# Turning three small vectors into rows with the matrix engine before they are written to DRAM

## The chip, the cores and the metric

The kernel runs on 1 core of one Trainium2 chip. The metric is the device time of one execution in microseconds (us); lower is better. The kernel was tuned already.

## The reference, cut to what matters

The program is a transformer block whose normalisations and residual additions are scaled and shifted by a condition vector `c`: linear attention, then a gated feed-forward net (S = 2048 tokens, D = 1024, F = 3584).

```python
mod = (silu(c) @ w_mod).reshape(1, 6, 1, D)
sa, ca, ga, sb, cb, gb = (mod[:, i] for i in range(6))
h = layernorm(x) * (1 + ca) + sa
x = x + ga * A(h, wqkv, wo)          # A: linear attention; it uses z = sum over the tokens of phi(k)
h = layernorm(x) * (1 + cb) + sb
x = x + gb * B(h, w_gate, w_up, w_down)   # B: silu(h @ w_gate) * (h @ w_up) @ w_down
```

Three vectors of 1024 numbers matter here: `ga`, `gb` and `z`. Each is computed as columns (element 128 m + p on partition p, column m), but is needed as one row that is repeated on all 128 partitions.

## The kernel before

A vector goes from columns to a repeated row by way of DRAM: write the 128x8 columns, wait until they have landed, read the row back with a broadcast. All DMAs are issued by one queue, that of the sync engine (SP), in program order; `wait_for("sp", ...)` makes that queue stand.

```python
def mod_cols(c0, first=None):                 # column sums: 16 matmuls of one column, into bank 6
    for m in range(NDT):
        for i in range(2):
            P.pe("matmul", out=PS[:, 6, c0 + m:c0 + m + 1], lhsT=MHL[:, i, m * 128:(m + 1) * 128],
                 rhs=ONES[:, 0:1], start=mcol_first[0], stop=(i == 1), skip_group_check=True)
            mcol_first[0] = False

def z_mm(st):                                 # z is summed in bank 6 too
    for hg in range(NHG):
        P.pe("matmul", out=PS[:, 6, 32 + hg:33 + hg], ...)   # arguments cut

def mod_fin_row(c0, i, dst):
    P.dve("tensor_copy", out=MROW[:, i, :], in_=PS[:, 6, c0:c0 + 8])
    wr = P.dma("mdw%d" % i, MDR[i].rearrange("(m p) -> p m", p=128), MROW[:, i, :], allow_slow_non_contiguous=True)
    P.wait_for("sp", [wr])
    P.dma("mdr%d" % i, dst[:], MDR[i].unsqueeze(0).to_broadcast([128, D]))
# ... cut: phases that project q and k. ga is made in the last of their four chunks:
add(s3, 2, lambda: mod_cols(0))
add(s3, 5, lambda: mod_fin_row(0, 0, GA_B))
# ... then z
P.dve("tensor_copy", out=ZCOL[:], in_=PS[:, 6, 32:40])
zw = P.dma("zw", ZDR[0].rearrange("(g p) -> p g", p=128), ZCOL[:], allow_slow_non_contiguous=True)
P.wait_for("sp", [zw])
P.dma("zr", ZB[:], ZDR[0:1, :].to_broadcast([128, D]))
P.dma("wo", WO[:], wov)
# ... cut. The first chunk (of four) of the feed-forward net:
for ft in range(NFT):                         # 28 steps of 16 matmuls, 3.45 us each
    q = 14 * ch + ft // 2
    # 8 matmuls with GUG[q % 4], 8 with GUU[q % 4], then the activation and the product (cut)
    if ft % 2 == 1 and q + 4 < 14 * NCH:
        gu_load(q + 4)                        # 1 MB of gate/up weights into the buffer just freed
    if ch == 0 and ft % 2 == 0 and ft < 14:
        P.dma("wd%d" % (ft // 2), ...)        # 1 MB of down weights (arguments cut)
    if ch == 0 and ft == 3:
        mod_cols(8)
        mod_fin_row(8, 1, GB_B)               # gb; first used after ft 27
```

Four gate/up buffers turn over: the load issued after step ft (odd) is used first in step ft + 7, some 20 us later. A helper makes an engine that touches a PSUM bank wait for the last use of that bank by every other engine.

## Time and profile before

| | before |
|---|---|
| time, median of the first 3 runs | 847.46 us (847.26 to 847.69) |
| the execution that the profile shows | 850.55 us, span 848.2 us |
| TensorE (PE) busy | 98% of the span |
| write of gb, issue to landing | 18.0 us for 2 KB |
| write of ga, issue to the next issue | 13.8 us for 2 KB |
| write of z, issue to landing | 10.4 us for 4 KB |

The second row of the table deserves a look: the execution in the profile took 3 us longer than the timed runs. I shall come back to it.

From the page of before: its span, the busy time, share and count of instructions of each engine, and the shares of the engines in the chain of work that ended last.

```profile
span 848.2 us, 10377 instructions
...
PE 835.3 (98%) x4287; PEld 385.3 (45%) x4287; DVE 296.1 (35%) x624; ACT 211.7 (25%) x363; POOL 39.7 (5%) x51
...
PE 93%; DMA 4%; DVE 2%; SPq 0%; issue 0%; POOL 0%; ACT 0%; DVEq 0%; ACTq 0%
...
```

PE is the limit nearly everywhere, so what counts is where PE stands. The waits of PE in before give the waiting engine, whom it waited for, the total, the number of waits and the longest.

```profile
...
PE ps L178 <- DMA guu_115<-in_B_w_up_dram: 5.4, 1, 5.4
...
PE ps L178 <- DVE mrow L178: 1.3, 1, 1.3
...
```

These are the only waits for the parts that the change touches. The first is for a gate/up load. Here is the sync queue of before in order of time (start, time to issue, what was issued):

```profile
...
273.20 0.86 SPq L178 DMA_DIRECT2D mod_row<-mrow  x1
291.20 0.34 SPq L178 DMA_DIRECT2D gb_b<-mod_row  x1
...
292.12 0.45 SPq L966 DMA_DIRECT2D gug_111<-in_B_w_gate_dram  x1
292.61 4.38 SPq L966 DMA_DIRECT2D guu_115<-in_B_w_up_dram  x1
...
```

The write of gb is issued at 273.20 us, just after the load of ft 3, and the queue issues nothing more until 291.20. The gate/up load after ft 5, which PE allowed near 278.6 us, when it was through with ft 5, is issued at 292.12. The timeline of PE shows what comes of it; in brackets is the idle time just before and its releaser:

```profile
...
297.56 1.89 PE L178 MATMUL ps<-h2t,guu_114 128*128 128x512 bf16 x8
304.82 3.59 PE L178 MATMUL ps<-h2t,gug_111 128*128 128x512 bf16 x8 [5.37 <-DMA guu_115<-in_B_w_up_dram]
308.21 2.19 PE L178 MATMUL ps<-h2t,guu_115 128*128 128x512 bf16 x8
310.24 1.89 PE L178 MATMUL ps<-h2t,gug_111 128*128 128x512 bf16 x8
...
```

PE idles 5.37 us. After that eight matmuls take 3.59 us, where eight take 1.89 us before and later. The stretch from 299 to 313 us of before, in the view by windows (length; busy time and instructions of PE, its weight loads, VectorE, ScalarE and GpSimd; granted clock; share of the DMA engines; GB/s):

```profile
...
299.00:313.00 14.00, 8.63 (x32) 3.35 (x30) 1.37 (x2) 1.19 (x2) 0.00 (x0) 0.76 1.12 333
...
```

The granted clock was 0.76. From the start of the group at 297.56 to the end of this disturbance the loss is 7.5 us: the ends of groups overlap with the next, and undisturbed a group of eight starts every 1.727 us, so these 32 matmuls should take 6.91 us from start to start and take 14.40 (297.56 to 311.96). The second wait, for the copy of ga out of bank 6, is 1.29 us long in PE's timeline of before:

```profile
...
115.31 3.61 PE L178 MATMUL ps<-wqk,ht 128*128 128x512 bf16 x16
120.21 0.25 PE L178 MATMUL ps<-ones,pk_87 128*128 128x1 bf16 x4 [1.29 <-DVE mrow L178]
...
```

The small matmuls at 120.21 us add to z in bank 6. They may not go on until VectorE has copied ga's columns out of the same bank, and VectorE has that copy behind other work.

### The profile page before, as it was taken

The page shows a single profiled execution, that of the slowest core. Times are in us where ns is not written, and L with a number is a line of the kernel's source. Part 1 is how long each engine was busy: PE and PEld are TensorE (multiplying, and loading weights), DVE is VectorE, ACT ScalarE, POOL GpSimd, SP SyncE. Part 2 cuts the span into 40 slices and gives each one's busy share as a digit, 9 for nine tenths or more (in the row PEclk, how much of TensorE's full clock was granted, in tenths as well). Part 3 has the DMA queues.
Part 4 walks back from the last instruction along what each step waited for, and adds up shares of the span by engine and source line. Part 5 has one row for each costly group of instructions (what it writes and reads, how often), then busy time and mean ns, then how long its engine had stood idle before and what let it go on. Part 6 is the DMA issues. An engine that isn't in the chain of part 4 may idle for free.

```text
span 848.2 us, 10377 instructions
## 1 busy us (share of the span) xinstructions
PE 835.3 (98%) x4287; PEld 385.3 (45%) x4287; DVE 296.1 (35%) x624; ACT 211.7 (25%) x363; POOL 39.7 (5%) x51
## 2 busy tenths in 40 slices
PE   8999999999999979999999999999999999999998
PEld 4544444444444434444444444444444444444444
DVE  4677966476984211111122111112211112122111
ACT  5677753223333111110111110111111101111101
POOL 1000000000050000020000002000000200000000
PEclk9899999999999989999999999999999999999999
DMA  9792321877195299540255554025555303553000
GB/s 311 221 315 50 67 80 14 222 205 260 39 249 183 36 338 293 155 112 26 63 149 149 149 152 115 19 85 158 156 156 154 67 26 106 149 148 100 1 25 25
DMA packets 176462, 113.00 MB, mean 133 GB/s; under 512 B 35616, under 2 KB 159648, under 8 KB 176416
## 3 DMA queue, kind: packets, MB, share of 16 engines
q1 hardware_dynamic: 176416, 112.35, 47.5%
q8 instruction: 33, 0.54, 0.3%
q14 instruction: 13, 0.11, 0.1%
HBM read 100.67 MB, written 4.33 MB: 124 GB/s over the span
## 4 chain that ended last, share of the span: by engine, by line
PE 93%; DMA 4%; DVE 2%; SPq 0%; issue 0%; POOL 0%; ACT 0%; DVEq 0%; ACTq 0%
PE ps L178 93%; DMA mod_row<-mrow 2%; DMA guu_115<-in_B_w_up_dram 1%; DMA xres<-in_A_x_dram 1%; DVE acc L178 0%; DVE xres L178 0%; SPq L966 0%; SPq L178 0%; DVE mhl L178 0%; POOL rstd L178 0%; DVE stats L178 0%; DVE mv L178 0%; ACT mw L178 0%; ACT e_92 L178 0%; DVE ve L178 0%
## 5 line engine op out<-in xcount | busy, mean ns | idle before, releaser
L178 DVE TENSOR_TENSOR at<-sg,ps 128x512 bf16<-128x512 bf16 x112 | 77.0, 688 | 305.3 <-PE ps L178 305.3
L178 ACT ACTIVATE sg<-ps 128x512 bf16<-128x512 f32 x112 | 66.9, 597 | 318.4 <-PE ps L178 318.4
L178 PE MATMUL ps<-wd_a,at 128*128 128x512 bf16 (+2 forms) x528 | 115.9, 373 | 0.0
L178 PE MATMUL ps<-wd_b,at 128*128 128x512 bf16 (+2 forms) x396 | 88.3, 373 | 0.0
L178 PEld LDWEIGHTS ps<-wd_a,at 128*128 128x128 bf16 x528 | 51.1, 98 | 59.8
L178 DVE TENSOR_TENSOR ut<-att,gb_b 128x512 bf16<-128x512 bf16 (+1 forms) x32 | 14.5, 454 | 164.8 <-ACT att L178 164.8
L178 ACT ACTIVATE att<-ps 128x512 bf16<-128x512 f32 (+1 forms) x32 | 19.0, 594 | 179.7 <-PE ps L178 179.7
L178 PE MATMUL ps<-h2t,gug_111 128*128 128x512 bf16 x224 | 54.6, 388 | 5.4 <-DMA guu_115<-in_B_w_up_dram 5.4
L178 PE MATMUL ps<-ht,wqk 128*128 128x512 bf16 x256 | 59.1, 387 | 0.0
L178 PEld LDWEIGHTS ps<-wd_b,at 128*128 128x128 bf16 x396 | 38.3, 98 | 44.7
L178 PE MATMUL ps<-wqk,ht 128*128 128x512 bf16 x256 | 58.5, 384 | 0.0
L178 PE MATMUL ps<-mw,pqt 128*128 128x512 bf16 x256 | 56.2, 379 | 0.1
L178 PE MATMUL ps<-h2t,guu_115 128*128 128x512 bf16 x224 | 53.2, 381 | 0.0
L178 PE MATMUL ps<-h2t,guu_113 128*128 128x512 bf16 x224 | 52.9, 379 | 0.0
L178 PE MATMUL ps<-h2t,gug_110 128*128 128x512 bf16 x224 | 52.9, 379 | 0.0
L178 PE MATMUL ps<-h2t,guu_114 128*128 128x512 bf16 x224 | 52.9, 379 | 0.0
L178 PE MATMUL ps<-h2t,gug_109 128*128 128x512 bf16 x224 | 52.9, 379 | 0.0
L178 PE MATMUL ps<-h2t,guu_116 128*128 128x512 bf16 x224 | 52.9, 379 | 0.0
L178 PE MATMUL ps<-h2t,gug_112 128*128 128x512 bf16 x224 | 52.9, 379 | 0.0
L178 POOL TENSOR_SCALAR h2t<-h2t,modcol 128x512 bf16<-128x512 bf16 x32 | 27.0, 857 | 404.0 <-DMA h2t<-xn_117 404.0
L178 ACT ACTIVATE e_92<-ps 128x512 bf16<-128x512 f32 x56 | 33.6, 599 | 29.2 <-PE ps L178 26.3
L178 PEld LDWEIGHTS ps<-mw,pqt 128*128 128x128 bf16 x256 | 24.9, 98 | 29.7 <-DVE xres L178 0.2
(117 smaller groups left out, 708.2 us busy)
## 6 DMA issues: line engine op xcount, KB each, us to landing
gug_109<-in_B_w_gate_dram SPq DMA_DIRECT2D x14, 512.0 KB, 4.0
guu_113<-in_B_w_up_dram SPq DMA_DIRECT2D x14, 512.0 KB, 5.2
gug_110<-in_B_w_gate_dram SPq DMA_DIRECT2D x14, 512.0 KB, 4.0
guu_114<-in_B_w_up_dram SPq DMA_DIRECT2D x14, 512.0 KB, 5.3
gug_111<-in_B_w_gate_dram SPq DMA_DIRECT2D x14, 512.0 KB, 4.0
guu_115<-in_B_w_up_dram SPq DMA_DIRECT2D x14, 512.0 KB, 5.3
gug_112<-in_B_w_gate_dram SPq DMA_DIRECT2D x14, 512.0 KB, 4.1
guu_116<-in_B_w_up_dram SPq DMA_DIRECT2D x14, 512.0 KB, 5.3
```

The costliest lines, as they stand in the source:

```text
L178: return getattr(e, method)(**kw)
```

## The change

The intent: a tiny matmul with the identity turns the 128x8 columns into 8 rows of 128; VectorE copies them out, and the DMA writes 8 contiguous runs (256 B each for ga and gb, 512 B for z) instead of 1024 elements. With it come four changes of order: ga's columns go to bank 7, apart from z in bank 6; their copy comes two slots earlier; the load of `wo` goes ahead of z's write; gb's write is issued after ft 5 instead of ft 3. The other column sums change bank or columns to fit, and the tile UT moves by 2 KB to make room.

```diff
--- before.py
+++ after.py
@@ -348,6 +348,8 @@
         MHL = T("mhl", 196 * KB, [128, 2, D], BF16)
         STGX = [T("stgx%d" % i, (72 + 16 * i) * KB, [128, NDT, D], BF16) for i in range(2)]
         GTMP = T("gtmp", 184 * KB, [128, 2, 512], FP32)
+        MR8 = T("mr8", 205 * KB, [128, 2, 128], BF16)
+        ZR8 = T("zr8", 205 * KB + 512, [128, 128], FP32)
         KVT = T("kvt", 188 * KB, [128, NHG, 128], BF16)
         ZSEL = T("zsel", SM + 7168, [128, 288], BF16)
         SILUF = T("siluf", SM + 7744, [128, NDT], FP32)
@@ -363,7 +365,7 @@
         GUU = [T("guu%d" % i, GU_OFF[i] + 4096, [128, NDT, 256], BF16) for i in range(4)]
         XN2 = T("xn2", 168 * KB, [128, NDT, 4, 128], BF16)
         H2T = T("h2t", 176 * KB, [128, NDT, 512], BF16)
-        UT = T("ut", 204 * KB, [128, 2, 512], BF16)
+        UT = T("ut", 202 * KB, [128, 2, 512], BF16)
         ATT = T("att", 190 * KB, [128, 2, 512], BF16)
         SG = T("sg", 184 * KB, [128, 2, 512], BF16)
         JUNK = T("junk", 186 * KB, [128, D], BF16)
@@ -650,12 +652,11 @@
             P.dve("tensor_copy", out=MHL[:, 0, :], in_=ACC[:])
             P.dve("tensor_tensor", out=MHL[:, 1, :], in0=ACC[:], in1=MHL[:, 0, :], op=ALU.subtract)
 
-        def mod_cols(c0, first=None):
+        def mod_cols(bank, c0):
             for m in range(NDT):
                 for i in range(2):
-                    P.pe("matmul", out=PS[:, 6, c0 + m:c0 + m + 1], lhsT=MHL[:, i, m * 128:(m + 1) * 128],
-                         rhs=ONES[:, 0:1], start=mcol_first[0], stop=(i == 1), skip_group_check=True)
-                    mcol_first[0] = False
+                    P.pe("matmul", out=PS[:, bank, c0 + m:c0 + m + 1], lhsT=MHL[:, i, m * 128:(m + 1) * 128],
+                         rhs=ONES[:, 0:1], start=(m == 0 and i == 0), stop=(i == 1), skip_group_check=True)
 
         def z_mm(st):
             for hg in range(NHG):
@@ -663,16 +664,20 @@
                      rhs=ONES[:, 0:1], start=mcol_first[0], stop=(st == NST - 1), skip_group_check=True)
                 mcol_first[0] = False
 
-        def mod_fin_col(c0, idx, plus_one):
-            P.dve("tensor_copy", out=MODTMP[:, 0:8], in_=PS[:, 6, c0:c0 + 8])
+        def mod_fin_col(bank, c0, idx, plus_one):
+            P.dve("tensor_copy", out=MODTMP[:, 0:8], in_=PS[:, bank, c0:c0 + 8])
             if plus_one:
                 P.dve("tensor_scalar", out=MODTMP[:, 0:8], in0=MODTMP[:, 0:8], scalar1=1.0, scalar2=None,
                       op0=ALU.add)
             P.dve("tensor_copy", out=MODCOL[:, idx, :], in_=MODTMP[:, 0:8])
 
-        def mod_fin_row(c0, i, dst):
-            P.dve("tensor_copy", out=MROW[:, i, :], in_=PS[:, 6, c0:c0 + 8])
-            wr = P.dma("mdw%d" % i, MDR[i].rearrange("(m p) -> p m", p=128), MROW[:, i, :], allow_slow_non_contiguous=True)
+        def mod_row_a(bank, c0, i):
+            P.dve("tensor_copy", out=MROW[:, i, :], in_=PS[:, bank, c0:c0 + 8])
+
+        def mod_row_b(bank, i, dst):
+            P.pe("matmul", out=PS[0:NDT, bank, 0:128], lhsT=MROW[:, i, :], rhs=IDENT[:], start=True, stop=True)
+            P.dve("tensor_copy", out=MR8[0:NDT, i, :], in_=PS[0:NDT, bank, 0:128])
+            wr = P.dma("mdw%d" % i, MDR[i].rearrange("(m p) -> m p", p=128), MR8[0:NDT, i, :])
             P.wait_for("sp", [wr])
             P.dma("mdr%d" % i, dst[:], MDR[i].unsqueeze(0).to_broadcast([128, D]))
 
@@ -787,17 +792,15 @@
         for kt in range(NDT):
             add(s3, 4 + kt, lambda kt=kt: macc(STG, kt))
         add(s3, 14, macc_split)
-        add(s3, 2, lambda: mod_cols(0))
-        add(s3, 5, lambda: mod_fin_row(0, 0, GA_B))
+        add(s3, 2, lambda: mod_cols(7, 0))
+        add(s3, 3, lambda: mod_row_a(7, 0, 0))
+        add(s3, 6, lambda: mod_row_b(7, 0, GA_B))
         chunk(1, s1)
         chunk(2, s2)
         chunk(3, s3)
         phi_flush()
 
         P.dve("tensor_copy", out=ZCOL[:], in_=PS[:, 6, 32:40])
-        zw = P.dma("zw", ZDR[0].rearrange("(g p) -> p g", p=128), ZCOL[:], allow_slow_non_contiguous=True)
-        P.wait_for("sp", [zw])
-        P.dma("zr", ZB[:], ZDR[0:1, :].to_broadcast([128, D]))
         P.dma("wo", WO[:], wov)
         P.dve("tensor_copy", out=ZHL[:, 0, :], in_=ZCOL[:])
         P.dve("tensor_tensor", out=ZHL[:, 1, :], in0=ZCOL[:], in1=ZHL[:, 0, :], op=ALU.subtract)
@@ -823,6 +826,14 @@
                   scale=MODCOL[:, 1, dt:dt + 1])
             P.dve("scalar_tensor_tensor", out=G[:, dt, h * 512:(h + 1) * 512], in0=PS[:, bank, :],
                   scalar=MODCOL[:, 0, dt:dt + 1], in1=GTMP[:, i, :], op0=ALU.mult, op1=ALU.add)
+
+        def z_row():
+            for i in range(2):
+                P.pe("matmul", out=PS[0:NHG, 6, 0:128], lhsT=ZHL[:, i, :], rhs=IDENT[:], start=(i == 0), stop=(i == 1))
+            P.dve("tensor_copy", out=ZR8[0:NHG, :], in_=PS[0:NHG, 6, 0:128])
+            zw = P.dma("zw", ZDR[0].rearrange("(g p) -> g p", p=128), ZR8[0:NHG, :])
+            P.wait_for("sp", [zw])
+            P.dma("zr", ZB[:], ZDR[0:1, :].to_broadcast([128, D]))
 
         def den():
             for hg in range(NHG):
@@ -899,8 +910,9 @@
                 g_evac(ev)
                 ev += 1
             if g == 0:
-                mod_cols(8)
-                mod_fin_col(8, 2, True)
+                z_row()
+                mod_cols(7, 0)
+                mod_fin_col(7, 0, 2, True)
             if g == 1:
                 den()
             if 6 <= g <= 9:
@@ -979,9 +991,8 @@
                 if st == 4:
                     macc_split()
             if st == 6:
-                mcol_first[0] = True
-                mod_cols(0)
-                mod_fin_col(0, 3, False)
+                mod_cols(6, 0)
+                mod_fin_col(6, 0, 3, False)
             if 8 <= st <= 15:
                 macc(STGX[1], st - 8)
                 if st == 15:
@@ -1018,8 +1029,10 @@
                     wt = WD_A[:, 4 * i:4 * i + 4, :] if i < 4 else WD_B[:, 4 * i - 16:4 * i - 12, :]
                     P.dma("wd%d" % i, wt, wdv[:, 4 * i:4 * i + 4, :])
                 if ch == 0 and ft == 3:
-                    mod_cols(8)
-                    mod_fin_row(8, 1, GB_B)
+                    mod_cols(6, 0)
+                    mod_row_a(6, 0, 1)
+                if ch == 0 and ft == 5:
+                    mod_row_b(6, 1, GB_B)
                 if nxt is not None and 4 <= ft < 8:
                     ln2_xn(4 * nxt + (ft - 4))
             if nxt is not None:
```

## The prediction

> **What bounds the kernel now.** TensorE: on the page PE is busy 98% of 848.2 us and is 93% of the chain. After start-up the waits name two larger PE holes: 1.3 us for the copy into mrow, 5.4 us for the DMA of guu_115. The chain in time puts them at 118.9-120.2 and 299.4-304.8 us.
>
> **What the change does.**
>
> 1. gb. In before the sync queue issues the element-wise write at 273.2 us and stands until it lands, 18.0 us later (2.1% of the chain). The gate/up load that PE allowed at about 278 us is issued at 292.1 and lands at 304.8; PE was ready at 299.4. Then the timeline shows about ten matmuls at 427 ns instead of 216, and the windows a granted clock of 0.76 over 299-313 us. Start to start, the 32 matmuls from 297.56 to 311.96 us take 14.40 us instead of 6.91: 7.5 us lost, 5.4 idle, 2.0 slow clock. The Trainium skill ("TensorE: Matmul & The Clock Gate", Part 1) says an idle window halves the clock until the array has been busy for a few us; the trace agrees.
> After: the write is 8 runs of 256 B, issued behind the load of ft 5, near 279 us. It queues behind that 1 MB and part of a wd load. From 6 MB issued in 292-313 us, 3.6 us per MB, I estimate 4-7 us to landing. The next gate/up load, allowed at 285 us, is delayed by 2 us at most, with 20 us before its use. Both losses go.
>
> 2. ga. Its columns move to bank 7, so the z sums in bank 6 no longer wait for the copy of mrow: start to start, 115.31-120.21 us becomes 3.45 us, 1.45 saved. Its write took 13.8 us for 2 KB on quiet queues; the Trainium skill ("DMA: Bandwidth & Descriptors", Rules for kernel authors) says a strided last dimension becomes one descriptor per element; this agrees. It shortens, but ga's first use is at 160 us: no gain.
>
> 3. z. The write takes 10.4 us and ScalarE waits 15.2 us for zb, but PE has no hole from 120.2 to 204 us: five banks cover it. The load of wo now goes ahead of z (about 137, not 149 us), so the write queues behind 2 MB until about 147; zb comes 1-2 us earlier. The reciprocal's write, no longer behind wo, falls from 8.7 us, and VectorE's 6.8 us wait for rb mostly goes. None of this moves PE.
>
> **Added.** Four small matmuls, three 8x128 copies; from small matmuls' start spacing (25-60 ns), 0.3 us of PE with waits.
>
> **Sum.** 847.46 - 7.5 - 1.45 + 0.3 = 838.8 us, range 837.3 to 842.5. Faster by over 2%: 0.01; within 2%: 0.97; slower by over 2%: 0.02.
>
> **What shows it right or wrong.** Waits: PE's for guu_115 and mrow gone, ScalarE's for zb still near 14 us. DMA issues: mod_row writes 2-7 us, z_row 6-10 us though contiguous, recip_den well under 8.7. Windows: granted clock 1.00 around 300 us. Chain: PE unbroken from about 28 us but for VectorE pieces.
>
> **What would make it wrong.** The gb write stays slow behind the loads and part of the stall comes back later in the first chunk, where the loads need about 300 GB/s (338 was reached): +2 to 7 us. New PE waits for zhl or mrow: up to 1 us. VectorE, busy 93% in 204-226 us, takes the 1.45 us back.

## The result, and the profile after

| | before | after |
|---|---|---|
| median, same session | 847.36 us (845.13 to 847.69, 4 runs) | 841.66 us (841.52 to 842.84, 4 runs) |
| ratio | | 0.9941 (0.9922 to 0.9961) |
| span in the profile | 848.2 us | 839.7 us |

Ratios and their 95% intervals lie nearer to the ratio of the mean times than to that of the medians quoted beside them. The change gains 0.6%, and the time lies near the upper end of the predicted range.

The page of after, the same three lines:

```profile
span 839.7 us, 10390 instructions
...
PE 832.7 (99%) x4291; PEld 384.4 (46%) x4291; DVE 296.6 (35%) x627; ACT 211.9 (25%) x363; POOL 39.7 (5%) x51
...
PE 95%; SPq 2%; DMA 1%; DVE 1%; ACT 0%; issue 0%; ACTq 0%; DVEq 0%
...
```

The waits of PE in after: the two of before that the change aimed at are not among them, and the longest is a wait of the start-up.

```profile
...
PE ps L178 <- DMA cs_57<-in_c_dram: 2.2, 1, 2.2
PE ps L178 <- DVE mv L178: 0.6, 2, 0.4
...
```

The sync queue of after, around the write of gb:

```profile
...
278.54 0.94 SPq L178 DMA_DIRECT2D mod_row<-mr_99  x1
283.18 0.35 SPq L178 DMA_DIRECT2D gb_b<-mod_row  x1
...
284.67 0.38 SPq L978 DMA_DIRECT2D gug_114<-in_B_w_gate_dram  x1
...
```

It stands for 4.6 us (278.54 to 283.18) instead of 18.0, and the next gate/up load is issued at 284.67, as early as PE allows it. PE's timeline of after around the added matmul of gb, and the stretch from 299 to 313 us:

```profile
...
275.54 1.89 PE L178 MATMUL ps<-h2t,guu_117 128*128 128x512 bf16 x8
277.36 0.22 PE L178 MATMUL ps<-ident,mrow 128*8 128x128 bf16 x1
277.51 1.90 PE L178 MATMUL ps<-h2t,gug_114 128*128 128x512 bf16 x8
...
```

```profile
...
299.00:313.00 14.00, 14.00 (x67) 6.35 (x65) 2.88 (x5) 2.39 (x4) 0.00 (x0) 1.00 1.05 309
...
```

PE works through at full clock: 67 matmuls in the same 14 us, where before had 32. Around the write of ga in after:

```profile
...
114.92 3.61 PE L178 MATMUL ps<-wqk,ht 128*128 128x512 bf16 x16
...
118.47 0.24 PE L178 MATMUL ps<-ones,pk_88 128*128 128x1 bf16 x4
118.64 0.22 PE L178 MATMUL ps<-ident,mrow 128*8 128x128 bf16 x1
118.79 1.90 PE L178 MATMUL ps<-wqk,ht 128*128 128x512 bf16 x8
...
```

The hole before the sums of z is gone. The four matmuls `ident,mrow` and `ident,zhl` are not free. From start to start, ga's adds 0.22 us (118.47 to 118.79 us, where 0.10 us separated these two groups before), gb's 0.24 us (1.97 instead of 1.73), and z's two, read in the same way, 0.31 us: 0.77 us in all. Finally the sync queue of after from ga to z:

```profile
...
121.22 0.30 SPq L178 DMA_DIRECT2D mod_row<-mr_99  x1
122.43 0.34 SPq L178 DMA_DIRECT2D ga_b<-mod_row  x1
134.93 0.38 SPq L178 DMA_DIRECT2D wo<-in_A_wo_dram  x1
138.91 0.29 SPq L178 DMA_DIRECT2D z_row<-zr_100  x1
143.62 0.33 SPq L178 DMA_DIRECT2D zb<-z_row  x1
...
```

The write of ga now takes 1.2 us on quiet queues (before: 13.8). The pages' counts of DMA packets under 512 B, 35616 before and 32536 after, differ by about the 3 x 1024 elements that are gone: each element had been a packet of its own. The write of z, issued at 138.91, lands just before 143.6 us; `wo`, issued at 134.93 ahead of it, landed 8.5 us later, near 143.4. The Trainium skill ("DMA: Bandwidth & Descriptors", Queues, rings and completion order) says that each DMA engine consumes a queue's descriptors in ring order. This trace agrees: the short write ended with the 2 MB in front of it.

The two traces balance. 0.4 us come from a start-up that happened to be earlier (the sums of z that begin at 115.10 us in before begin anywhere from 113.95 to 115.58 us in the 14 traces of this document), 1.45 from bank 6, 7.5 from the stall, and 0.77 go to the small matmuls: 8.6 us, against spans 8.5 us apart. The timed runs, however, are only 5.7 us apart. So something in the pair of traces is not typical, and the experiments had to find it as well as check the parts.

### The profile page after: what moved, and what is told of

Read it like the earlier page. It is cut to its first block, busy times and chain, and to the rows that moved or that the text cites. A ratio compares the mean times of both kernels' runs of the same rounds, so it can differ in the third digit from the quotient of the medians. Undisturbed runs are those within 1.5% of the kernel's fastest.

```text
span 839.7 us, 10390 instructions
## 1 busy us (share of the span) xinstructions
PE 832.7 (99%) x4291; PEld 384.4 (46%) x4291; DVE 296.6 (35%) x627; ACT 211.9 (25%) x363; POOL 39.7 (5%) x51
## 2 busy tenths in 40 slices
DMA packets 173391, 113.02 MB, mean 135 GB/s; under 512 B 32536, under 2 KB 156576, under 8 KB 173344
## 4 chain that ended last, share of the span: by engine, by line
PE 95%; SPq 2%; DMA 1%; DVE 1%; ACT 0%; issue 0%; ACTq 0%; DVEq 0%
PE ps L178 95%; SPq L178 2%; DMA xres<-in_A_x_dram 1%; DVE acc L178 0%; ACT ht L178 0%; DVE xres L178 0%; DVE mhl L178 0%; DVE stats L178 0%; ACT mw L178 0%; ACT e_92 L178 0%; DVE ve_72 L178 0%; DVE ut L178 0%; DVE mv L178 0%; ACT rl L178 0%; DVE mean_70 L178 0%
```

## The experiments

Theory A was: the form of the write (1024 elements) is what is slow; it makes the sync queue stand, so a gate/up load comes late, and this stall differs in size from run to run. Rivals were: the gain is due to the later place of gb's write, not its form; the DMA engines are blocked by the elements whether the queue stands or not; z's row counts as well. Each run was timed in 5 rounds, which with the profiled execution gives 6 runs; the kernel before ran 11 times in each of three sessions (each on a chip of its own). Means are quoted where small differences matter. The diffs below are cut to the lines that matter.

### before_again: the spread of the kernel before

No edit.

> The kernel before, unchanged, for its own spread. The page of before came from an execution of 850.55 us; its timed runs were 845.1 to 847.7 us. Theory A (the stall at the late gate/up load varies from run to run, and the page caught a long one): spans of single runs spread over 2 us or more, with a lower mean granted clock in the longer ones, and the new trace shows an idle time of 2 to 5 us at the stall. Theory B (the time outside the span, or taking a profile, makes the difference): the stall in the new trace is again 5.4 us idle and 7.5 us lost, and every run's span lies within 0.5 us of 848. Ratio 1.000.

It took 848.23 us median (845.80 to 850.68), ratio 1.0006 (0.9981 to 1.0031). The eleven runs of before beside it went from 845.14 to 851.23 us, with spans of 843.3 to 849.4 us; the shortest had a mean granted clock of 0.998, the longest of 0.992. The new profile caught a run of 846.25 us, span 844.4. PE's timeline of before_again at the stall, and its stretch from 299 to 313 us:

```profile
...
298.04 1.89 PE L178 MATMUL ps<-h2t,guu 128*128 128x512 bf16 x8
302.94 1.90 PE L178 MATMUL ps<-h2t,gug 128*128 128x512 bf16 x8 [3.00 <-DMA guu<-in_B_w_up_dram]
...
```

```profile
...
299.00:313.00 14.00, 10.99 (x52) 4.82 (x51) 2.06 (x3) 1.79 (x3) 0.00 (x0) 1.00 1.12 325
...
```

The same stall is 3.00 us idle here, and afterwards the clock stays at 1.00: 3.2 us lost in place of 7.5. The kernel is the same; the write of gb took 16.2 us in this run and 18.0 in the other. That is theory A, and it says what was wrong with the first profile: it had caught one of the long runs. The timed runs agree: of the 39 runs of before in the three sessions, the 13 with a mean granted clock of 0.998 had spans of 841.8 to 844.4 us, the 6 with 0.992 spans of 846.8 to 849.4 us. (Slow clock during the start-up counts in this mean too; 13 of the 14 traces show 3.4 or 6.8 us of it.)

### gb_row: the row write of gb alone

```diff
-                    mod_fin_row(8, 1, GB_B)            # at ft 3, after mod_cols(8)
+                    mod_row_a(8, 1)                    # at ft 3: copy the columns out of bank 6
+                if ch == 0 and ft == 5:
+                    mod_row_b(1, GB_B)                 # small matmul, copy, write of 8 rows, read
```

> The kernel before with the row write of gb alone (small identity matmul after ft 5). If the stall at the late gate/up load is the whole of the large term: PE's wait for guu is gone, and the time falls by the stall of a typical run (4.5 to 7.5 us) less 0.25 us for the matmul: 840 to 843 us. If contention of the loads mattered more than the standing queue: a stall of 1 to 5 us stays in the first chunk, and the time falls by under 3 us.

843.11 us median (842.46 to 845.07), mean 843.39, just above the expected 840 to 843; ratio 0.9950 (0.9929 to 0.9971). PE's waits for the gate/up loads are gone. Against the mean of the 17 runs of before on this chip (847.67) it gains 4.3 us, so with the 0.24 us of the matmul the stall of an average run is about 4.5 us. This one part gives most of the gain of the whole change.

### ga_bank7: bank 7 for ga's columns alone

```diff
-        add(s3, 2, lambda: mod_cols(0))
-        add(s3, 5, lambda: mod_fin_row(0, 0, GA_B))
+        add(s3, 2, mod_cols7)                          # the same 16 matmuls into PS[:, 7, 0:8]
+        add(s3, 5, lambda: mod_fin_row(0, 0, GA_B, 7)) # copy at the old place, element-wise write
```

> The kernel before with ga's columns in bank 7, its copy at the old place (slot 5) and its element-wise write kept. If the shared bank was the cause of the 1.3 us hole: the hole is gone, 1.3 to 1.45 us faster, about 846.0 us. If the late place of the copy was the cause: the hole stays and nothing changes. If a shift of 1.45 us is taken back by the stall at the late load: the hole is gone, but the time changes by less than 0.7 us.

847.66 us median (846.12 to 849.30), ratio 1.0001 (0.9980 to 1.0022). The interval is 3.5 us wide, so the time alone cannot show a gain of 1.3 us: inconclusive. The trace says more. The hole at the sums of z is gone although the copy stands in its old slot, so the shared bank was its cause. But PE waited at two other places in this execution, once for the product `g`, which waits for z:

```profile
...
144.47 10.53 PE L178 MATMUL ps<-pk,xres 128*128 128x512 bf16 x48
155.75 4.49 PE L178 MATMUL ps<-pk,xres 128*128 128x512 bf16 x20 [0.74 <-DVE g L178]
```

At their undisturbed spacing the forty-eight matmuls from 144.47 us would have been followed by the next at 154.83 us; it starts at 155.75. z's element-wise write had taken 12.7 us here (10.4 in the first trace of before). The other wait is the old one, and here 3.94 us of idle time came with a slow clock (0.76 over 299 to 313 us):

```profile
...
297.37 1.89 PE L178 MATMUL ps<-h2t,guu 128*128 128x512 bf16 x8
303.20 3.60 PE L178 MATMUL ps<-h2t,gug 128*128 128x512 bf16 x8 [3.94 <-DMA guu<-in_B_w_up_dram]
...
```

### z_row: z's row alone (the result was wrong)

```diff
-        zw = P.dma("zw", ZDR[0].rearrange("(g p) -> p g", p=128), ZCOL[:], allow_slow_non_contiguous=True)
-        P.wait_for("sp", [zw])
-        P.dma("zr", ZB[:], ZDR[0:1, :].to_broadcast([128, D]))
             if g == 0:
+                z_row()                                # in bank 6, ahead of mod_cols(8) in bank 6
                 mod_cols(8)
```

> The kernel before with z's row alone, and the load of wo ahead of it. Off the critical path: zb's wait falls from 15.2 to 11-14 us, VectorE's wait for rb from 6.8 to about 1 us, and the time does not fall; it rises by the two small matmuls, 0.2 to 0.4 us: 847.5 us. If z was on the critical path: faster by 1 us or more.

The output was wrong. My edit kept `mod_cols(8)` in bank 6, where it adds to columns that the new matmul had just filled; the change avoids that by moving the sums to bank 7. (gb_z, which keeps the two in different banks, is correct; how the values went wrong was not traced further.) The values do not change the order of the work, so the times are told all the same: 849.99 us median (847.39 to 851.88), ratio 1.0024 (0.9998 to 1.0050), no gain. The expected 847.5 us was missed by 2.5; the interval includes no change, and what made these runs long is not shown beyond a stall of 7.0 us in the trace. VectorE's copy of z's rows also held PE for 0.37 us, because both used bank 6. A clean trial is gb_z below.

### after_again: the changed kernel in a later session

No edit.

> The changed kernel, unchanged, beside its parts on one chip. Both theories: 841.0 to 842.5 us, a spread of at most 1.5 us (no stall at the late load, so nothing that varies with it), and 1.3 us or so faster than gb_row's 843.1.

841.58 us median (840.88 to 843.42), mean 841.75, ratio to before 0.9941 (0.9914 to 0.9969). The eleven runs of before beside it spread over 7.7 us, these six over 2.5, more than the expected 1.5; five of the six lie within 0.9 us.

### gb_z: gb's and z's rows

The edit is gb_row and z_row together, with z's two matmuls in bank 7.

> gb's row write and z's row write together (the two matmuls of z in bank 7); ga's columns still in bank 6 and written as elements. Replaces z_row, whose result was wrong[...]. Theory A and B both: the 1.3 us hole at mrow stays, so z's row alone gains nothing; it costs 0.3 us, so about 0.3 us above gb_row, 843.4 us. If z were the limit by itself: 1 us or more below gb_row.

The result is correct: 843.14 us median (842.24 to 843.86), mean 843.02. That is 4.1 us below before on this chip (847.12), much as gb_row gained on its own in another session (4.3), and it is 1.3 us above after. z's row alone adds no gain that these runs can show. after_again differs from gb_z by ga's part, apart from which bank z's matmuls and the sums after them use, and the 1.3 us fit ga's bank (1.45) less its small matmul (0.22).

### gb_ga: gb's row and ga's bank 7, without the other rows

The edit is gb_row and ga_bank7 together; ga and z are still written as elements.

> gb's row write and ga's columns in bank 7 together; ga and z still written as elements. Theory A (z's slow write becomes the next limit once bank 7 lets PE run ahead, as the trace of ga_bank7 with PE waiting 0.7 us for g suggests): PE waits for g between 150 and 156 us, 0.5 to 2 us, and the time is 842.5 to 843.5 us, within 0.7 us of gb_row. Theory B (z's row is worth nothing, as predicted): no wait for g, and the time is that of after less 0.5 us for the three small matmuls that it lacks, about 841.2 us.

840.98 us median (840.40 to 841.59), mean 841.00: 0.75 us below after_again. PE waits for `g` nowhere. Theory B of this expectation holds in this execution, but with little room: the first `g` was finished at about 151.9 us, and PE needed its bank at 153.35. z's row widens that room. In the trace of after the first `g` was finished at about 149.6, and PE needed its bank at 154.66.

### gb_col_defer: elements, but the queue does not stand

```diff
                 if ch == 0 and ft == 3:
                     mod_cols(8)
-                    mod_fin_row(8, 1, GB_B)
+                    gb_wr = mod_col_w(8, 1)            # copy, element-wise write, no wait
+                if ch == 0 and ft == 15:
+                    mod_col_r(gb_wr, 1, GB_B)          # wait, then read
```

> The kernel before with gb still written as 1024 elements at the old place, but the wait for it and the read of gb_b moved from ft 3 to ft 15, so that the sync queue doesn't stand. Theory A (what stalls PE is the sync queue that stands on the write, so that the next load is issued 14 us late): the stall is gone, about 843 us, as gb_row. Theory B (the 1024 elements block the DMA rings, and the next load lands late even if issued in time): the next gate/up load, issued near 278 us, lands after 298 us, and PE still waits 1 to 5 us for it.

843.07 us median (842.47 to 845.96), mean 843.55: about the time of gb_z (843.02). Its sync queue and PE's timeline:

```profile
...
272.98 0.98 SPq L178 DMA_DIRECT2D mod_row<-mrow  x1
...
278.91 0.37 SPq L974 DMA_DIRECT2D gug<-in_B_w_gate_dram  x1
279.32 5.59 SPq L974 DMA_DIRECT2D guu<-in_B_w_up_dram  x1
284.95 10.19 SPq L178 DMA_DIRECT2D wd_a<-in_B_w_down_dram  x1
...
```

```profile
...
297.66 1.89 PE L178 MATMUL ps<-h2t,guu 128*128 128x512 bf16 x8
300.10 1.90 PE L178 MATMUL ps<-h2t,gug 128*128 128x512 bf16 x8 [0.55 <-DMA guu<-in_B_w_up_dram]
...
```

Both theories have a part. The gate/up load is issued at 278.91 us, in time, and PE's idle time shrinks to 0.55 us: the standing queue was the larger part of the trouble. But the load itself was slow: its gate half landed 18.3 us after its issue (8.3 us was the longest of that kind in after), its up half, for which PE waits, 20.7 us (9.8), and the queue took 5.59 and 10.19 us to issue the up half and the load after it. PE got its weights only just too late. In this trace the elements hold up what is queued behind them even when the queue does not stand.

### gb_row_early: rows, at the old place

```diff
-                if ch == 0 and ft == 3:
-                    mod_cols(8)
-                    mod_fin_row(8, 1, GB_B)
+                if ch == 0 and ft == 1:
+                    mod_cols(8)
+                    mod_row_a(8, 1)
+                if ch == 0 and ft == 3:
+                    mod_row_b(1, GB_B)
```

> gb as 8 rows, but issued where before issues its elements: column sums at ft 1, small matmul and write at ft 3. Theory A (the form of the write makes it slow): the write issued near 273 us lands in 4 to 6 us behind the load of ft 3, the next loads are issued in time, no stall: 843 us, as gb_row, and a spread under 2.5 us. Theory B (the later place in the queue did it): PE still waits for a gate/up load and the time stays above 845 us.

843.16 us median (842.47 to 844.04), mean 843.19, ratio 0.9962. There is no stall. From its sync queue:

```profile
...
272.19 1.09 SPq L178 DMA_DIRECT2D mod_row<-mr  x1
276.81 0.36 SPq L178 DMA_DIRECT2D gb_b<-mod_row  x1
...
```

Issued where before issues its elements, the write lets the next DMA go after 4.6 us instead of 18.0.

### gb_col_late: elements, at the new place

```diff
-                if ch == 0 and ft == 3:
+                if ch == 0 and ft == 5:
                     mod_cols(8)
                     mod_fin_row(8, 1, GB_B)
```

> gb still as 1024 elements, but issued behind the load of ft 5, where the changed kernel issues its rows. Theory A (form): the write stands 16 to 18 us from about 280 us on, the load of ft 7 is issued near 299 us instead of 285 and lands near 311, PE is ready at about 306: again 3 to 6 us idle, 846 to 850 us. Theory B (place): no stall, about 843 us.

844.51 us median (844.08 to 846.24), mean 844.81, ratio 0.9979 (0.9957 to 1.0001). Its sync queue and PE's timeline:

```profile
...
278.58 3.48 SPq L178 DMA_DIRECT2D mod_row<-mrow  x1
295.25 0.34 SPq L178 DMA_DIRECT2D gb_b<-mod_row  x1
...
296.18 0.45 SPq L966 DMA_DIRECT2D gug<-in_B_w_gate_dram  x1
...
```

```profile
...
303.60 1.89 PE L178 MATMUL ps<-h2t,guu 128*128 128x512 bf16 x8
307.31 1.90 PE L178 MATMUL ps<-h2t,gug 128*128 128x512 bf16 x8 [1.81 <-DMA guu<-in_B_w_up_dram]
...
```

The write holds the queue for 16.7 us, as theory A says, and the stall is back, one gate/up load later. But it is 1.81 us of idle time and not the 3 to 6 that I had expected, the clock stays full, and the time is below the expected 846 to 850; why the stall is smaller here was not tested. By the means the later place alone gains 1.7 us on before (846.48), with an interval that just reaches no change; the rows at the old place gain 3.3. So the form is the cause; the place decides how much of it is seen. gb_row_early is 1.6 us faster than gb_col_late in the same rounds.

### gb_ga_again and after_third: which version is the fastest

No new edits: gb_ga and the changed kernel side by side on a third chip.

> gb's row and ga's bank 7 alone, again, to see whether the version without the other rows is really the faster: 0.5 to 0.8 us below the changed kernel of the same rounds (three small matmuls less), about 841.0 us, with a spread under 1.5 us. If the 0.75 us of the first time was chance, the two are equal within 0.2 us.

> The changed kernel, unchanged, beside gb_ga_again on one chip: 841.3 to 842.0 us median.

gb_ga_again took 841.60 us median (840.97 to 842.43), mean 841.68; after_third 842.22 (841.44 to 843.36), a little above the expected 841.3 to 842.0, mean 842.29; before had a mean of 846.48. gb_ga was 0.75 us faster in one session and 0.61 us in the other. The three small matmuls that it lacks stand in the trace of after with 0.53 us. Two sessions agree with it, but with six runs on each side, spread over more than 1 us, I call this likely and not shown. gb_ga_again is 1.5 us below gb_row_early; the two differ by ga's bank and by the place of gb's rows.

## Why the prediction was right or wrong

1. **The stall at the gate/up load.** Right in mechanism, wrong in size; this is the term of the sum that failed. I put it at 7.5 us, read from one execution. Comparing before with the kernel that has gb as rows on the same chip, and adding back the small matmuls, an average run of before loses 4.5, 4.6 and 3.5 us there (847.67 - 843.39 + 0.24; 847.12 - 843.02 + 0.55; 846.48 - 843.19 + 0.24; the 95% intervals of these differences reach some 2 us to either side). The profile came from an execution of 850.55 us, while the timed runs had a median of 847.46; both numbers were before me, and I used the stall of the one and the time of the other. The four traces with this stall (gb written as elements at ft 3) show why runs differ:

| trace | gb's write, issue to release | PE idle | granted clock, 299 to 313 us | lost from start to start |
|---|---|---|---|---|
| before_again | 16.2 us | 3.00 us | 1.00 | 3.2 us |
| ga_bank7 | 17.4 us | 3.94 us | 0.76 | 6.9 us |
| before | 18.0 us | 5.37 us | 0.76 | 7.5 us |
| z_row | 18.4 us | 5.18 us | 0.88 | 7.0 us |

A write that is 1 or 2 us longer becomes about as much more idle time, and then PE's slow clock adds 1.7 to 2.8 us or nothing. The Trainium skill ("TensorE: Matmul & The Clock Gate", Part 1) gives an idle window of about 3.4 us, not tied to the program's start, after which the clock is halved. The traces agree with such a window, but not with a length of idle time that would be safe. The same stretch of before and of z_row in the view by windows, PE idle throughout in both:

```profile
...
302.00:304.50 2.50, 0.00 (x0) 0.00 (x0) 0.00 (x0) 0.00 (x0) 0.00 (x0) 0.50 1.08 337
...
```

```profile
...
302.00:304.50 2.50, 0.00 (x0) 0.00 (x0) 0.00 (x0) 0.00 (x0) 0.00 (x0) 1.00 1.04 344
...
```

PE had been idle since about 299.4 us in both, and yet the clock (third number from the end) is at half in before and full in z_row. Read with finer windows, it was at half from 302.0 to 308.8 us in before, 302.1 to 308.9 in ga_bank7 and 304.5 to 307.9 in z_row. It was halved 2.5, 2.8 and 5.2 us after PE fell idle, while 3.00 us of idle time in before_again left it full. So it matters where the idle time falls in the window, and not only how long it is: of the three that slowed, z_row, with 5.18 us of idle time, lost less to the clock than ga_bank7 with 3.94.

2. **Bank 6.** Right: 1.45 us by the traces; in the sessions 1.5 us (gb_z against after_again, 1.27, with the small matmul's 0.22 added back) and 1.5 us (gb_row_early against gb_ga_again). With six runs on a side these are good to some tenths of a microsecond at best. Alone, ga_bank7 could not show it, because the spread of the stall hid it.

3. **z.** Nearly right. Nothing of z moved PE in before, after, gb_ga or gb_ga_again. "Five banks cover it" is true by 1.6 us in the trace of before (the first `g` done at 154.4 us, its bank needed at 156.0), and bank 7 takes most of that. In the one trace of ga_bank7 the room was used up, and PE was 0.9 us late. My estimate that the write queues behind `wo` was right, but it landed near 143.5 us, not 147, since `wo` was issued 2 us earlier and took 8.5 us. So z's write took 4.7 us, not 6 to 10, and the read of zb was issued 5.1 us earlier than before, not 1 to 2. ScalarE's wait for zb fell to 11.2 us, not 14. The reciprocal's write fell from 8.7 to 1.6 us and VectorE's wait for rb from 6.8 to 0.6, as predicted, and none of that reached the time.

4. **Added work.** 0.77 us in the trace instead of 0.3: each small matmul costs PE 0.15 to 0.24 us from start to start. I had taken the spacing of a stream of small matmuls, and these stand alone between others.

5. **What I had named as risks.** The stall did not return later in the chunk, VectorE did not take back the 1.45 us, and PE did not wait for zhl or mrow. The range had been drawn with these risks named; the size of the stall was not among them. That the measured time still fell inside the range, near its upper end, is in part luck.

The sum with the measured terms is 4.2 (the mean of the three) + 1.45 - 0.77 = 4.9 us. Measured as means: 5.0 us in the first session, 5.4 and 4.2 us in the other two.

## What to carry to other kernels

A tiny transfer can cost a large stall where the issuing queue waits for it and other loads stand behind; look at what the queue does between two issues, and at the form of the write, not at its bytes. Before a hole in a trace is put into a prediction, check that the traced execution took the same time as the timed runs, since one stall can cost more than twice as much in one run as in another (here 3.2 to 7.5 us), part of it through a clock that slows or does not. A wait that costs nothing has a margin: know it before another part of the change makes the engine in front faster.

## What the Trainium skill lacked or had wrong

- "DMA: Bandwidth & Descriptors" (Rules for kernel authors) says that a strided last dimension becomes one descriptor per element, but gives no time for a small store of that kind. Here, on quiet queues, 1024 elements of 2 bytes took 13.8 us and 1024 of 4 bytes 10.4 us, against 1.2 us for the same 2 KB as 8 runs of 256 B.
- The same page gives no figure for what such a store does to what follows it in the queue. In gb_col_defer the halves of a gate/up load issued behind it landed after 18.3 and 20.7 us, with 8.3 and 9.8 us as the longest of their kinds in after, and the queue took 5.59 and 10.19 us to issue the up half and the load after it.
- "TensorE: Matmul & The Clock Gate" (Part 1) calls the ramp a penalty under 1% of a span and its start variable. That agrees, but the section does not say that a stall of about the window's length makes the times of one kernel spread: before ran from 843.51 to 851.23 us over three sessions, and the changed kernel, without the stall, from 840.88 to 843.42 us. Nor does it say how much of its idle window must be idle: here the clock was halved 2.5 and 2.8 us after PE fell idle (before, ga_bank7), and after 3.00 us it was still full (before_again).
- The same page gives start-to-start times of streams of small matmuls (not below about 25 ns) and a latency for a single matmul; it does not say what a lone small matmul adds between large ones. Here one adds 0.15 to 0.24 us from start to start.
